# Values later in each pass, and the last row blocks' chains earlier, in a two-layer attention and MLP kernel bound by ScalarE's exponentials

## The chip, the cores and the metric

One core of one Trainium2 chip. The metric is the time of one execution on the device in microseconds (us). Every execution also comes with the span of the core (from its first to its last instruction, about 1.8 us less) and its mean granted TensorE clock. All executions here are in the fast state; they still differ by some us, and much of this document is about why.

## The reference

Two layers of the same weights, each an attention and an MLP with residuals, over x of 2048 x 448 in bf16, 16 heads of 28:

```python
x = x + A(layernorm(x), wqkv, wo)     # softmax(q k^T / sqrt(28)) v, 16 heads, then @ wo
x = x + B(layernorm(x), w1, b1, w2, b2)   # relu(x @ w1 + b1)^2 @ w2 + b2, 448 -> 1792 -> 448
x = x + A(layernorm(x), wqkv, wo)
x = x + B(layernorm(x), w1, b1, w2, b2)
```

## The kernel before

The kernel is written as several streams of operations with a rank each. A planner in the program itself (it runs when the program is built) merges them into one fixed order per engine: of the operations that can start, the earliest, and at a tie the lower rank. So a constant moves thousands of instructions.

A *unit* is the scores of one head for 512 (key, query) columns in a PSUM bank. Three units fill a score tile (sc), and ScalarE takes their exponential in one instruction into a pt tile. VectorE takes a single unit now and then, by a polynomial of seven instructions (vi, vm, vh, pd). A *pass* is one group of four heads and one row block of 256 rows (128 in the last four blocks of the second layer). Its values are summed into one bank (oT), which VectorE then copies out to oT_sb (the *eviction*). When all four groups of a row block are done, its *chain* runs: projection, add to x, norm, MLP, add to x, store.

PSUM: two score tiles of three banks and two single banks. The single banks serve oT, the chain's matmuls (mt, tp), VectorE's units and *filler* (useless matmuls that keep TensorE busy).

```python
HEAT = 0.74        # filler matmuls when TensorE was busy for less than this
LASTP = 3.9        # rank of the last row block's chain
HOLD = 3           # values of a pass start at this many eighths of it
NPT = 11           # pt tiles
...
blocks = [[(0, 2), ..., (14, 2)], [(0, 2), ..., (10, 2), (12, 1), (13, 1), (14, 1), (15, 1)]]
...
def apart(i, now):                 # may VectorE take unit i?
    ...
    near = p_next[0] is not None and e_now[0] >= p_next[0] - NEAR_U
    want[0] = sum(r.when() is not None and r.when() <= now for r in R_m) < 1 + near
    return not want[0]             # not if too few single banks are free
...
def p_stream():                    # values, rank 2
    for pi, (l, qb, g, kbs, first, last) in enumerate(passes):
        ...
        hold = todo[0 if end else min(HOLD * len(todo) // 8, len(todo) - 1)]
        ...                        # wait until the scores of step `hold` have their exponentials
...
    if len(norm_done[l, qb]) == G:                       # V_PRIO, VectorE's exponentials: 3.8
        pl.spawn(LASTP if (l, qb) == (1, len(blocks[1]) - 1) else 4 + 0.1 * qb, chain(l, qb))
```

The softmax here doesn't subtract the row's maximum and nothing guards it: scores larger than these inputs give would overflow.

## Time and profile before

| | before |
|---|---|
| time, median of the first 3 runs | 939.75 us (939.41 to 942.1) |
| time, mean of 74 later runs | 939.95 us |
| span of the profiled run | 935.4 us, clock 0.993 |
| exponentials on ScalarE / units on VectorE | 663 / 59 |
| after ScalarE's last exponential | 22.6 us |

The lines that the prediction shows are not repeated. One more view is needed for later: ScalarE's timeline after its last exponential (start, duration, instruction, idle time before and what ended it).

```profile
912.91 0.60 ACT L897 ACTIVATE r<-sc 128x512 bf16<-128x512 f32 x1
...
914.63 0.59 ACT L421 COPY xnT<-sc 128x512 bf16<-128x512 bf16 x1
920.63 0.60 ACT L897 ACTIVATE r<-sc 128x512 bf16<-128x512 f32 x1 [5.41 <-PE sc L471]
921.69 0.59 ACT L421 COPY xnT<-tp 128x512 bf16<-128x512 bf16 x1 [0.46 <-PE tp L412]
```

Each xnT is the normed input of one row block's MLP. Two are made after the last exponential, and the first instruction belongs to a third block's MLP: three chains are still open when the exponentials end. In the trace, 136 first-layer and 42 second-layer matmuls start after that point.

### The profile page before, as it was taken

The numbers are of one execution on the slowest core, as the hardware profiler recorded it, in microseconds if no ns is written. First come the engines' busy times: TensorE is split into PE (matmuls) and PEld (weight loads), VectorE is DVE, ScalarE is ACT, GpSimd is POOL, SyncE is SP. The second block draws the span as 40 slices with busy tenths as digits, with TensorE's granted clock in tenths as the row PEclk, the third lists the DMA queues.
The fourth block names the chain that finished last, engine by engine and source line by source line (L and its number), as shares of the span: only waits on it lengthen the run. The fifth ranks groups of instructions, "written<-read, shape, count | busy, mean of one in ns | idle before, by whom it ended". The sixth has DMA issues, their size and how long they took to land.

```text
span 935.4 us, 28412 instructions
## 1 busy us (share of the span) xinstructions
PE 831.2 (89%) x12637; PEld 440.7 (47%) x12637; DVE 615.7 (66%) x1291; ACT 905.0 (97%) x683; POOL 41.3 (4%) x84
## 2 busy tenths in 40 slices
PE   8999878899888898888989999789888999888888
PEld 4555434344444444444445444444344444545556
DVE  6755676666677776766678564667677476666565
ACT  5999999999999999999999999999999999999992
POOL 4100000100000000000000000000000000000000
PEclk9999999999999999999999999999999999999999
DMA  9000010000000000000000000011000000000100
GB/s 277 10 2 1 3 43 13 13 9 13 14 10 12 13 14 8 13 14 1 1 2 2 1 2 2 14 38 30 18 14 18 18 18 18 17 22 12 25 11 16
DMA packets 34471, 18.39 MB, mean 20 GB/s; under 512 B 18474, under 2 KB 33899, under 8 KB 34348
## 3 DMA queue, kind: packets, MB, share of 16 engines
q1 hardware_dynamic: 34348, 16.58, 6.4%
q8 instruction: 98, 1.61, 0.7%
q14 instruction: 25, 0.20, 0.1%
HBM read 14.26 MB, written 2.07 MB: 17 GB/s over the span
## 4 chain that ended last, share of the span: by engine, by line
ACT 72%; issue 14%; PE 13%; DVE 1%; POOL 0%; ACTq 0%; DVEq 0%
ACT pt L663 72%; PE mt L471 4%; PE sc L645 3%; PE oT L766 2%; PE sc L471 2%; PE mt L281 1%; PE mt L946 1%; PE tp L412 0%; DVE x_sb L861 0%; DVE vh L698 0%; ACT Q_sb L486 0%; POOL rstd L393 0%; DVE xn L438 0%; DVE vi L676 0%; DVE xnT L423 0%
## 5 line engine op out<-in xcount | busy, mean ns | idle before, releaser
L663 ACT ACTIVATE pt<-sc 128x1536 bf16<-128x1536 f32 x663 | 892.0, 1777 | 3.6 <-PE sc L645 3.1
L645 PE MATMUL sc<-Q_sb,K_sb 32*128 32x256 bf16 (+1 forms) x5082 | 285.2, 261 | 84.1 <-ACT pt L663 77.6
L645 PEld LDWEIGHTS <-K_sb 32*128 32x128 bf16 x5256 | 130.4, 92 | 261.6 <-issue 251.4
L766 PE MATMUL oT<-pt,V_sb 128*32 128x256 bf16 (+1 forms) x4476 | 159.0, 265 | 0.0
L471 PE MATMUL mt<-xnT,w 128*128 128x256 bf16 (+1 forms) x904 | 119.0, 268 | 5.0 <-DVE vi L676 3.0
L766 PEld LDWEIGHTS <-V_sb 128*32 128x32 bf16 x4608 | 91.5, 96 | 50.3 <-issue 45.6
L899 DVE TENSOR_SCALAR r<-mt 128x512 bf16<-128x512 f32 (+1 forms) x105 | 71.4, 680 | 48.1 <-PE mt L471 46.9
L471 PEld LDWEIGHTS <-w 128*128 128x128 bf16 x1008 | 79.5, 98 | 40.6 <-issue 31.8
L698 DVE SCALAR_TENSOR_TENSOR vh<-vh,vm 128x512 f32<-128x512 f32 x118 | 80.7, 684 | 1.4
L676 DVE TENSOR_SCALAR vi<-mt 128x512 int32<-128x512 f32 x59 | 40.8, 691 | 54.0 <-PE mt L645 53.9
L946 PE MATMUL mt<-xn,ident 128*128 128x448 bf16 x211 | 70.8, 359 | 3.6 <-DVE xn L438 1.4
L861 DVE TENSOR_TENSOR x_sb<-x_sb,mt 128x448 bf16<-128x448 bf16 x62 | 38.3, 618 | 48.5 <-PE mt L471 47.9
L471 PE MATMUL mt<-w,h 128*128 128x448 bf16 x224 | 53.7, 355 | 0.0
L392 POOL TENSOR_TENSOR ve<-mv,eps_t 128x2 f32<-128x2 f32 (+1 forms) x34 | 9.0, 264 | 873.1 <-DVE mv L374 801.2
L471 PE MATMUL mt<-w,V_sb 128*128 128x448 bf16 x196 | 46.5, 355 | 0.0
L789 DVE COPY oT_sb<-oT 128x256 f32<-128x256 f32 (+1 forms) x52 | 19.7, 379 | 37.1 <-PE oT L766 36.8
L703 DVE SCALAR_TENSOR_TENSOR pd<-vh,vi 128x512 bf16<-128x512 f32 x59 | 40.4, 685 | 0.7
L373 DVE BATCH_NORM_STATS2 st<-x_sb 128x6 f32<-128x448 bf16 x64 | 39.6, 619 | 1.3 <-DMA x_sb<-in_A_x_dram 0.6
L698 DVE SCALAR_TENSOR_TENSOR vh<-vm 128x512 f32<-128x512 f32 x59 | 40.2, 681 | 0.0
L492 DVE CAST K_sb<-mt 128x512 bf16<-128x512 f32 x30 | 20.7, 691 | 22.3 <-PE mt L471 22.1
L471 PE MATMUL mt<-xnT,wk 128*128 128x256 bf16 x240 | 34.1, 274 | 0.8 <-DVE vi L676 0.8
L471 PE MATMUL mt<-wo,oTn 128*128 128x448 bf16 x128 | 33.6, 368 | 0.4
(83 smaller groups left out, 643.4 us busy)
## 6 DMA issues: line engine op xcount, KB each, us to landing
rec<-scr SPq DMA_DIRECT2D x52, 128.0 KB
x_sb<-in_A_x_dram SPq DMA_DIRECT2D x8, 224.0 KB
out_dram<-x_sb SPq DMA_DIRECT2D x16, 112.0 KB
w<-in_B_w_dram SPq DMA_DIRECT2D x1, 1568.0 KB
w<-in_B_w_dram SPq DMA_DIRECT2D x1, 1344.0 KB
dn<-oT_sb SPq DMA_DIRECT2D x52, 4.0 KB
scr<-dn SPq DMA_DIRECT2D x52, 4.0 KB
rec<-scr SPq DMA_DIRECT2D x12, 64.0 KB
```

The costliest lines, as they stand in the source:

```text
L373: nc.vector.bn_stats(out=st[:, :], in_=x_sb[:, t0 + j, :])
L471: nc.tensor.matmul(box["t"][:, c0:c0 + n], lhsT=lhsT() if callable(lhsT) else lhsT, rhs=rhs, start=a, stop=b)
L492: nc.vector.tensor_copy(out=dst, in_=src)
L645: nc.tensor.matmul(dst[k][:, i * nt * P:(i + 1) * nt * P], lhsT=K_sb[l][rows, g, (kb + i) * P:(kb + i + 1) * P], rhs=Q_sb[rows, g, t0 * P: ...
L663: nc.scalar.activation(out=pt[:, 0:n], in_=gbuf[gi]["sc"][:, 0:n], func=AF.Exp, scale=float(np.log(2.0)) * 2.0 ** -23)
L676: nc.vector.tensor_scalar(out=box["i"][:, :], in0=src, scalar1=EXP_BIAS, scalar2=0.0, op0=ALU.add, op1=ALU.max)
L698: nc.vector.scalar_tensor_tensor(out=h[:, :], in0=src, scalar=b, in1=m, op0=ALU.add, op1=ALU.mult)
L703: nc.vector.scalar_tensor_tensor(out=pd[:, :], in0=h[:, :], scalar=b0, in1=i.bitcast(DT.float32), op0=ALU.add, op1=ALU.mult)
L766: nc.tensor.matmul(box["t"][DHP * hh:DHP * hh + DHP, 0:n], lhsT=V_sb[l][:, kb + i, 4 * g + hh, :], rhs=p[:, c0:c0 + n], start=begin and kb ...
L861: nc.vector.tensor_tensor(out=x_sb[:, tb, :], in0=x_sb[:, tb, :], in1=t[:, 0:D], op=ALU.add)
L899: nc.vector.tensor_scalar(out=r[:, 0:w], in0=t[:, 0:w], scalar1=0.0, scalar2=None, op0=ALU.max)
L946: nc.tensor.matmul(t[:, 0:D], lhsT=ident[:, :], rhs=xns[0][:, 0:D], start=True, stop=True)
```

## The change

The intent: hold the oT bank for a shorter time, so that chains and VectorE's exponentials find a free bank; and let the chains of the last row blocks go ahead of VectorE's exponentials, so that less of them is left at the end. By the edit this holds for three of the last four: they get ranks 3.4 to 3.6, below the 3.8 of VectorE's exponentials, while the last block's chain keeps 3.9, and so falls behind the other three, which it led before. Lines of the changed kernel stand five lower than those of the kernel before (L663 is L668).

```diff
-HOLD = 3
+HOLD = 5
+HOLD1 = 7
+NL = 4
+NLP = 3.8
+STOP = 0
+HSTOP = 0
...
-            hold = todo[0 if end else min(HOLD * len(todo) // 8, len(todo) - 1)]
+            hold = todo[0 if end else min((HOLD if nt == 2 else HOLD1) * len(todo) // 8, len(todo) - 1)]
...
-            pl.spawn(LASTP if (l, qb) == (1, len(blocks[1]) - 1) else 4 + 0.1 * qb, chain(l, qb))
+            pl.spawn(LASTP if (l, qb) == (1, len(blocks[1]) - 1) else NLP + 0.1 * (qb - len(blocks[1])) if l == 1 and qb >= len(blocks[1]) - NL else 4 + 0.1 * qb, chain(l, qb))
```

(Left out: STOP and HSTOP enter two conditions; at 0 they do nothing.)

More of the change, by code (lines that the diff above doesn't have):

```diff
@@ L588, in apart @@
         want[0] = False
-        if not LEAD <= len(gbuf) <= LAST or i + LAG > ends_at[units[i][0]]:
+        if len(units) - i < STOP or not LEAD <= len(gbuf) <= LAST or i + LAG > ends_at[units[i][0]]:
             return False
@@ L938, in heat @@
             short = HEAT - pl.load(WINDOW)
-            if short <= 0 or not s_left:
+            if short <= 0 or not s_left or len(units) - at[0] < HSTOP:
                 continue
```

## The prediction

> **What bounds the kernel now.** I read the page first (busy shares, then the groups), then the windows, then the timelines of ScalarE and VectorE at the end of the run.
>
> ```profile
> PE 831.2 (89%) x12637; PEld 440.7 (47%) x12637; DVE 615.7 (66%) x1291; ACT 905.0 (97%) x683; POOL 41.3 (4%) x84
> ...
> L663 ACT ACTIVATE pt<-sc 128x1536 bf16<-128x1536 f32 x663 | 892.0, 1777 | 3.6 <-PE sc L645 3.1
> ```
>
> ScalarE is busy 97% of a span of 935.4 us, and 892.0 us of its 905.0 are one group: 663 exponentials of 128x1536. A further 59 units of 128x512 get their exponential on VectorE (the group that writes pd, x59): 3 x 663 + 59 = 2048 units, all there are. TensorE's 89% is not a bound of the same kind: it is partly filler (211 matmuls of the identity, L946, and repeated score matmuls) and it waits 77.6 us for ScalarE by the list of waits.
>
> From the trace's records of the exponentials: the first ends at 17.2 us, the last at 912.8 us, and 650 of the 662 distances between successive ends average 1.343 us. So the span is 17.2 (start) + 662 x 1.343 = 889.3 + 6.3 lost + 22.6 (tail) = 935.4 us. Of the 6.3 us, 2.4 are in the start, at 25 to 28 us. The other 3.9 lie in four places, and the windows show what they have in common:
>
> ```profile
> 184.00:188.00 4.00, 3.83 (x47) 1.57 (x47) 0.69 (x4) 3.21 (x3) 0.00 (x0) 0.59 0.02 4
> 662.00:666.00 4.00, 4.00 (x31) 1.29 (x23) 3.03 (x7) 3.58 (x3) 0.00 (x0) 0.57 0.07 23
> 785.00:789.00 4.00, 4.00 (x50) 1.46 (x49) 1.25 (x3) 3.55 (x4) 0.00 (x0) 0.57 0.00 0
> 850.00:854.00 4.00, 3.73 (x65) 2.44 (x65) 2.56 (x6) 3.75 (x4) 0.00 (x0) 0.57 0.06 18
> ```
>
> The columns are busy time of PE, PEld, DVE, ACT, POOL, then the granted clock. In each the clock falls to 0.50 for 3.41 us, the scores come late, and ScalarE idles; from the exponentials' ends they cost 1.0, 1.3, 0.9 and 0.6 us. Each follows a quiet stretch of TensorE (busy 0.93 of 2.00 us at 180 to 182).
>
> The tail, from VectorE's timeline (start, duration, instruction):
>
> ```profile
> 915.21 0.29 DVE L789 COPY oT_sb<-oT 128x128 f32<-128x128 f32 x1
> ...
> 917.14 0.29 DVE L850 TENSOR_TENSOR oTn<-oT_sb,rec 128x128 bf16<-128x128 f32 x1
> 918.37 0.62 DVE L861 TENSOR_TENSOR x_sb<-x_sb,mt 128x448 bf16<-128x448 bf16 x1 [0.94 <-PE mt L471]
> 919.03 0.63 DVE L373 BATCH_NORM_STATS2 st<-x_sb 128x6 f32<-128x448 bf16 x1
> ...
> 929.22 0.62 DVE L861 TENSOR_TENSOR x_sb<-x_sb,sc 128x448 bf16<-128x448 bf16 x1 [1.40 <-PE sc L471]
> 932.06 0.62 DVE L861 TENSOR_TENSOR x_sb<-x_sb,sc 128x448 bf16<-128x448 bf16 x1 [2.22 <-PE sc L471]
> ```
>
> After the last exponential (912.8) it is one dependent chain: the last values, eviction at 915.21, reciprocal, output projection added at 918.37, norm, first MLP layer, second layer added at 932.06, store. The two adds at 929.22 and 932.06 are those of the last two row blocks: the chain of the last but one was still to do, and took TensorE from the last one.
>
> **What the Trainium skill says.** "ScalarE: Activation LUTs", section What ACT_TABLE_LOAD costs: an activation with immediate scale and bias takes 186 ns + 0.833 ns per element, and neighbours overlap by about 93 ns. For 1536 that is 1373 ns; the trace has 1343, which agrees, and 0.833 x 512 = 0.43 us is my estimate of what an exponential of 1024 saves. "TensorE: Matmul & The Clock Gate", section Part 1: The HAM clock gate: a free-running window of 3413 ns, and half clock after an idle one; the trace has four stretches of 3.41 us at 0.50, after windows busy only about half, so not fully idle ones. "PSUM — Partial Sum Buffer", section Specifications (TRN2): eight banks of 2 KiB. Here two score tiles take three each, so two single banks (mt, oT) serve values, chains, filler and VectorE's exponentials alike; no trace shows the size of PSUM, but the tiles' names show the sharing.
>
> **The change, part by part.** STOP and HSTOP are 0 and do nothing. The order of instructions of the two built programs gives the counts.
>
> *Values later.* A pass of 256 rows has 32 units, 10.7 exponentials, 14.3 us. Its oT bank was taken after 3/8 of them and held till eviction: between 100 and 500 us the median from the first value matmul to the eviction's end is 7.6 us. Starting at 5/8 removes 2/8 x 14.3 = 3.6 us of that, to about 4. A pass of 128 rows has 5.3 exponentials, 7.2 us; from its second of four steps to its last is half, another 3.6 us off a median of 4.4. The number of value matmuls stays at 4608. What the freed bank buys is that VectorE takes 63 units, not 59. ScalarE then has 661 exponentials of 1536 and one of 1024: 1 x 1.343 + 0.43 = **1.8 us less** on the bound. The four more on VectorE cost it some 4 x 4.0 us (0.69 + 0.42 + 0.42 + 4 x 0.68 = 4.25, pipelined a little), beside the bound: DVE is at 66%.
>
> *Filler.* 24 identity matmuls fewer (24 x 0.19 = 4.5 us), 105 repeated score matmuls more (at about 0.07 us, 7 us). TensorE's total grows by under 3 us, off the path.
>
> *Chains of the last four row blocks ahead of VectorE's exponentials.* Before, ScalarE had nine instructions of chains left after its last exponential, with two transposed inputs (xnT); after, five, with one. In TensorE's order only 15 second-layer matmuls of the last but one block are left behind the last value matmul; before, its whole first layer, too. I lay out the new tail with the old durations, E being the end of the last exponential. The last values need no wait for 56 first-layer matmuls any more (before: they ran at 914.53, 1.7 us after E); eviction at E + 0.8 (before E + 2.4). Then, however, the order puts the other block's 15 second-layer matmuls between the sum of denominators and the output projection. From eviction O: denominators until O + 0.9, 15 matmuls 2.85 us (926.18 to 929.02 in the old trace), projection 0.8, drain 0.2: the add starts at O + 4.75, where before it was O + 3.16. So 1.6 us are given back. Then add to xnT 3.9 us as before (918.37 to 922.28); 56 first-layer matmuls alone on TensorE at 0.056 us each, 3.2; last relu and square 1.4; second layer 3.05; add, store and its landing 3.3 (932.06 to 935.4). Sum: 0.8 + 4.75 + 3.9 + 0.1 + 3.2 + 1.4 + 3.05 + 3.3 = 20.5 us against 22.6: **2.1 us less**. One check: the last VectorE exponential. From its vi to its pd VectorE has 14 instructions of 8.0 us, and ScalarE from the same point 6 x 1.343 + 0.9 = 9.0 us less some 0.8 until vi starts, 8.2 us, so it ends just in time.
>
> *Lateness.* Bunching the values at the end of a pass loads TensorE unevenly. Charging each score, value and chain matmul with its old pace, 57 of the stretches from one score tile to the next hold over 1.6 us of TensorE work (before 38), and the greatest backlog, as an estimate from those paces, is 0.9 us (before 0.6) where a score may be about 0.9 late (1.343 less 0.4 for itself). I charge **0.5 us**.
>
> Sum: -1.8 - 2.1 + 0.5 = -3.4 us. 939.75 - 3.4 = 936.3, say **936.2 us**.
>
> **Rivals.** (1) *Clock dips decide.* They are worth 0.6 to 1.3 us each and depend on the phase of a free window, so four may be one or eight. For: the runs of before spread over 2.7 us, as much as the gain. With one dip the time would be 933, with eight, 940. By my sums, stretches of three score tiles with under 2.4 us of work go from six to eight, so slightly against us. (2) *Scores late behind the bunched values.* For: backlog 0.9 is the whole slack, and a half-clock stretch falling into such a bunch costs double. Against: ScalarE waits just 3.6 us for scores now. It would make 938 to 943. (3) *ScalarE waits for a buffer.* There are 11 pt tiles, and a pass now holds 8 before its first value matmul. For: three tiles are 4 us of slack, and a value step may wait for VectorE's share, 4 us and more. Against: no wait of ScalarE for oT exists now. If each of the 36 full passes of 256 rows lost 0.4 us, that is 14 us and the time 950. (4) *The tail gives nothing*, if the 15 matmuls and the last pd come later than I lay out: 938.
>
> **Range and chances.** The certain part is 1.8 us (counts). The tail is good for 0 to 4, dips for +-3, lateness for 0 to 4. In 8 of 10 cases I expect 931.8 to 940.8. Two per cent are 19 us: no term here comes near it, as the start, 660 exponentials at a fixed pace and a dependent tail remain. Faster by over 2%: 0.01; within: 0.98; slower: 0.01, for rival 3.
>
> **What would show it.** Right: 662 exponentials, pace 1.343; pd x63; hold of oT about 4 us; tail 20 to 21 us with the projection's add waiting for second-layer matmuls; no ACT wait for oT. Wrong: gaps between exponentials outside the half-clock stretches (rival 2), ACT waiting for PE's values (3), a tail of 22 us or more (4), or a number of half-clock stretches far from four (1). The prediction fails if the losses in mid-run come to under 1 or over 8 us.

## The result, and the profile after

| | before | after |
|---|---|---|
| time, median | 940.91 us (4 runs) | 935.56 us (4 runs, 934.47 to 936.68) |
| ratio | | 0.9944, 95% interval 0.9921 to 0.9967 |
| ratio when repeated (11 runs) | | 0.9954, 0.9937 to 0.9970 |
| span of the profiled run | 935.4 us, clock 0.993 | 934.9 us, clock 0.982 |

Ratios are the mean time of one kernel's fast runs over that of the other's of the same rounds, so not quite the ratio of the medians quoted. The change is 0.5% faster: inside the 2% band, inside the range, close to the predicted 936.2.

Yet the two profiles differ by only 0.5 us. Both numbers are right, and the clock tells why. The profiled run of before was one of its best (spans of its 74 later runs: 934.5 to 941.4, mean 938.0). From the page of the changed kernel:

```profile
PE 825.9 (88%) x12718; PEld 447.8 (48%) x12718; DVE 633.1 (68%) x1323; ACT 900.8 (96%) x678; POOL 41.5 (4%) x84
...
L668 ACT ACTIVATE pt<-sc 128x1536 bf16<-128x1536 f32 x662 | 890.3, 1739 | 6.3 <-PE sc L650 4.9
...
L708 DVE SCALAR_TENSOR_TENSOR pd<-vh,vi 128x512 bf16<-128x512 f32 x63 | 43.1, 685 | 1.7 <-PE oT L771 0.9
```

662 exponentials and 63 units on VectorE, as the order said. ScalarE's idle time ahead of exponentials rose from 3.6 to 6.3 us. The windows of the changed kernel (busy time of PE, PEld, DVE, ACT, POOL, then the granted clock) show where:

```profile
101.00:105.00 4.00, 3.62 (x52) 1.43 (x51) 2.82 (x6) 4.00 (x4) 0.00 (x0) 0.64 0.00 0
105.00:109.00 4.00, 4.00 (x45) 1.40 (x40) 2.06 (x4) 3.09 (x3) 0.00 (x0) 0.51 0.01 4
...
600.00:604.00 4.00, 3.73 (x45) 1.54 (x47) 3.00 (x6) 3.39 (x4) 0.00 (x0) 0.57 0.03 2
```

Before had four half-clock stretches of 3.41 us. This run has eight before the last exponential, three pairs (the first from 102.1 to 108.9 us) and two single ones. From the ends of the exponentials, the eight cost 5.9 us (before: four, 3.8 us), and all other gaps after the start 0.9 us.

The tail is the second surprise. VectorE's timeline, to be held against that of before in the prediction:

```profile
914.34 0.29 DVE L794 COPY oT_sb<-oT 128x128 f32<-128x128 f32 x1 [0.94 <-PE oT L771]
...
916.21 0.29 DVE L855 TENSOR_TENSOR oTn<-oT_sb,rec 128x128 bf16<-128x128 f32 x1
918.05 1.38 DVE L866 TENSOR_TENSOR x_sb<-x_sb,sc 128x448 bf16<-128x448 bf16 x2 [1.55 <-PE sc L476]
919.46 0.63 DVE L378 BATCH_NORM_STATS2 st<-x_sb 128x6 f32<-128x448 bf16 x1
...
931.57 0.62 DVE L866 TENSOR_TENSOR x_sb<-x_sb,mt 128x448 bf16<-128x448 bf16 x1 [1.88 <-PE mt L476]
```

The last exponential ends at 913.63. The eviction follows after 0.71 us (before 2.39). Then the two adds stand together: the other block's second layer and the last block's projection, the latter starts at 918.81, 4.47 us after the eviction (before 3.16), about as laid out. But from the input of the last MLP to its end TensorE is slow. Its timeline:

```profile
917.85 0.92 PE L476 MATMUL sc<-wo,oTn 128*128 128x448 bf16 x4
921.69 0.61 PE L417 MATMUL tp<-ident,xn 128*128 128x128 bf16 x4 [2.92 <-DVE xn L443]
922.97 1.87 PE L476 MATMUL mt<-xnT,w 128*128 128x128 bf16 x16 [0.67 <-ACT xnT L426]
924.63 3.62 PE L476 MATMUL sc<-xnT,w 128*128 128x128 bf16 x32
928.05 0.65 PE L476 MATMUL mt<-xnT,w 128*128 128x128 bf16 x8
928.53 0.35 PE L476 MATMUL mt<-b2w,one 128*128 128x448 bf16 x1
```

The 56 first-layer matmuls take 5.7 us from 922.97, not 3.2, after 2.92 us in which TensorE waited for the norm. The windows give the clock:

```profile
918.00:921.00 3.00, 0.77 (x5) 0.20 (x2) 2.05 (x4) 0.00 (x0) 0.54 (x2) 1.00 0.11 38
921.00:925.00 4.00, 2.63 (x24) 2.48 (x25) 0.40 (x1) 0.71 (x2) 0.20 (x1) 0.54 0.00 0
925.00:928.00 3.00, 3.00 (x31) 3.00 (x29) 0.85 (x2) 1.07 (x2) 0.00 (x0) 0.50 0.00 0
```

TensorE was busy for 0.77 of 3 us, and then it ran at half clock from 921.3 to 928.1 us: two stretches right in the last dependent chain. ScalarE's timeline shows that only one MLP input is made after the last exponential, where there were two:

```profile
913.74 0.38 ACT L902 ACTIVATE r<-sc 128x256 bf16<-128x256 f32 x1
922.34 0.59 ACT L426 COPY xnT<-tp 128x512 bf16<-128x512 bf16 x1 [8.22 <-PE tp L417]
924.88 0.60 ACT L902 ACTIVATE r<-mt 128x512 bf16<-128x512 f32 x1 [1.95 <-PE mt L476]
```

56 first-layer and 28 second-layer matmuls are left for after that point, against 136 and 42.

So the profiled pair balances to: start -0.3, exponentials -1.8, gaps between exponentials +2.9, tail -1.3, sum -0.5 us. The mean of many runs says -4.2 us of span (933.8 for 15 runs, 938.0 for 74). To compare kernels, the chance in the clock has to be taken out.

**Counting half-clock stretches in every run.** Each run's mean clock is on record, so (1 - clock) x span x 2 / 3.413 is its number of half-clock stretches. An estimate, by least squares over the 185 runs of all kernels here but hold7_lastp (one free constant for each kernel, one common slope): a stretch costs 0.79 us, standard error 0.04. The constant, the span with no stretch at all, is an extrapolation and called *fixed span* below: before 932.0, after 926.2 us, errors of 0.3 to 0.5. The change takes 5.9 us off the fixed span and adds 2.1 stretches (7.6 to 9.7 a run), 1.6 us; the sum is the measured -4.2. The common slope is a simplification: fitted one by one, the kernels' slopes run from 0.24 (cap59) to 1.24 (heat85), further apart than their errors (0.06 to 0.32) allow, and the own fits of before and after give 930.8 and 925.9 us, 4.9 apart with an error of 1.5. So fixed spans are good to about 1 us, not to 0.3.

### The profile page after: what moved, and what is told of

Same layout as the page of the kernel before. It is cut to its first block, busy times and chain, and to the rows that moved or that the text cites. A ratio compares the mean times of both kernels' runs of the same rounds, so it can differ in the third digit from the quotient of the medians.

```text
span 934.9 us, 28645 instructions
## 1 busy us (share of the span) xinstructions
PE 825.9 (88%) x12718; PEld 447.8 (48%) x12718; DVE 633.1 (68%) x1323; ACT 900.8 (96%) x678; POOL 41.5 (4%) x84
## 4 chain that ended last, share of the span: by engine, by line
ACT 69%; issue 17%; PE 10%; DMA 2%; DVE 1%; SPq 0%; POOLq 0%; POOL 0%; ACTq 0%
ACT pt L668 69%; PE sc L650 3%; PE mt L476 3%; DMA dn<-oT_sb 2%; PE oT L771 1%; PE sc L476 1%; PE mt L286 1%; PE mt L951 1%; PE tp L417 0%; DVE vh L703 0%; DVE st L378 0%; DVE x_sb L866 0%; DVE oT_sb L796 0%; DVE vi L681 0%; DVE dn L838 0%
## 5 line engine op out<-in xcount | busy, mean ns | idle before, releaser
L668 ACT ACTIVATE pt<-sc 128x1536 bf16<-128x1536 f32 x662 | 890.3, 1739 | 6.3 <-PE sc L650 4.9
L650 PE MATMUL sc<-Q_sb,K_sb 32*128 32x256 bf16 (+1 forms) x5194 | 292.3, 264 | 88.7 <-ACT pt L668 84.1
L771 PE MATMUL oT<-pt,V_sb 128*32 128x256 bf16 (+1 forms) x4468 | 153.6, 266 | 0.6 <-ACT pt L668 0.6
L476 PE MATMUL mt<-xnT,w 128*128 128x256 bf16 (+1 forms) x968 | 122.8, 265 | 5.2 <-DVE vi L681 1.6
L771 PEld LDWEIGHTS <-V_sb 128*32 128x32 bf16 x4608 | 94.6, 97 | 45.4 <-issue 40.8
L904 DVE TENSOR_SCALAR r<-mt 128x512 bf16<-128x512 f32 x110 | 74.6, 678 | 47.1 <-PE mt L476 46.3
L476 PEld LDWEIGHTS <-w 128*128 128x128 bf16 x1008 | 82.3, 100 | 40.4 <-issue 31.4
L703 DVE SCALAR_TENSOR_TENSOR vh<-vh,vm 128x512 f32<-128x512 f32 x126 | 86.2, 684 | 1.7
L951 PE MATMUL mt<-xn,ident 128*128 128x448 bf16 x187 | 63.1, 369 | 1.6 <-DVE xn L443 0.9
L443 DVE TENSOR_SCALAR xn<-x_sb,mv,rstd 128x448 bf16<-128x448 bf16 x64 | 23.5, 391 | 14.5 <-POOL rstd L398 14.1
L476 PE MATMUL mt<-xnT,wq 128*128 128x256 bf16 x240 | 33.1, 274 | 0.1
```

Source lines behind the costliest of these rows:

```text
L443: nc.vector.tensor_scalar(out=xn[:, 0:D], in0=x_sb[:, t0 + j, :], scalar1=mv[0][:, j, 0:1], scalar2=ln["r"][:, j:j + 1], op0=ALU.subtract, ...
L476: nc.tensor.matmul(box["t"][:, c0:c0 + n], lhsT=lhsT() if callable(lhsT) else lhsT, rhs=rhs, start=a, stop=b)
L650: nc.tensor.matmul(dst[k][:, i * nt * P:(i + 1) * nt * P], lhsT=K_sb[l][rows, g, (kb + i) * P:(kb + i + 1) * P], rhs=Q_sb[rows, g, t0 * P: ...
L668: nc.scalar.activation(out=pt[:, 0:n], in_=gbuf[gi]["sc"][:, 0:n], func=AF.Exp, scale=float(np.log(2.0)) * 2.0 ** -23)
L703: nc.vector.scalar_tensor_tensor(out=h[:, :], in0=src, scalar=b, in1=m, op0=ALU.add, op1=ALU.mult)
L771: nc.tensor.matmul(box["t"][DHP * hh:DHP * hh + DHP, 0:n], lhsT=V_sb[l][:, kb + i, 4 * g + hh, :], rhs=p[:, c0:c0 + n], start=begin and kb ...
```

## The experiments

Each is the changed kernel with the edit shown. Twelve runs were made beside the kernel before, in three calls on one chip each; each call has its own runs of the kernel before (24, 15 and 35). All results were correct.

| kernel | runs | median us | ratio to before (95%) | exponentials | stretches a run | fixed span | tail in its profile |
|---|---|---|---|---|---|---|---|
| before | 74 | 939.2, 940.9, 940.1 | 1 | 663 | 7.6 | 932.0 | 22.58 |
| after_again | 11 | 935.53 | 0.9954 (0.9937 to 0.9970) | 661 + 2/3 | 9.7 | 926.2 | 21.19 |
| chains_only | 14 | 939.58 | 0.9998 (0.9984 to 1.0012) | 663 | 7.0 | 931.7 | 22.60 |
| hold_only | 6 | 933.10 | 0.9929 (0.9903 to 0.9956) | 661 + 2/3 | 7.2 | 926.0 | 21.03 |
| hold128_only | 10 | 935.69 | 0.9951 (0.9930 to 0.9972) | 663 | 7.3 | 928.1 | 19.00 |
| hold256_only | 6 | 932.70 | 0.9932 (0.9907 to 0.9956) | 662 + 1/3 | 7.4 | 926.2 | 18.39 |
| cap59 | 11 | 936.46 | 0.9953 (0.9937 to 0.9970) | 663 | 8.7 | 927.4 | 19.49 |
| tail_warm | 6 | 932.24 | 0.9924 (0.9901 to 0.9946) | 661 + 2/3 | 7.7 | 924.8 | 18.63 |
| lastp | 6 | 933.14 | 0.9920 (0.9897 to 0.9944) | 661 + 2/3 | 9.5 | 924.0 | 18.90 |
| lastp_warm | 6 | 931.68 | 0.9916 (0.9888 to 0.9945) | 661 + 2/3 | 7.5 | 924.3 | 17.30 |
| heat85 | 9 | 936.03 | 0.9955 (0.9938 to 0.9972) | 665 | 1.6 | 932.5 | 19.41 |
| hold6_both | 22 | 937.40 | 0.9976 (0.9964 to 0.9989) | 660 + 2/3 | 11.0 | 927.2 | 19.64 |
| hold7_lastp | 5 | 978.59 | 1.0411 (1.0385 to 1.0437) | 659 + 2/3 | 18.9 | not fitted | 22.37 |

(The row after_again has the 11 runs of that call; its stretches and fixed span are those of all 15 runs of the changed kernel.)

The tails, cut at their dependent steps, in us; the half clock column is what overlaps the tail in that profile:

| | last exponential to eviction | to projection's add | to MLP input | to last square | to last add | to end | half clock |
|---|---|---|---|---|---|---|---|
| predicted | 0.8 | 4.75 | 3.9 | 4.7 | 3.05 | 3.3 | none |
| before | 2.39 | 3.16 | 3.91 | 5.54 | 4.24 | 3.34 | none |
| after | 0.71 | 4.47 | 4.12 | 6.77 | 1.88 | 3.34 | 6.8 us |
| chains_only | 1.39 | 7.77 | 3.89 | 4.33 | 1.88 | 3.33 | none |
| hold_only | 3.12 | 2.83 | 3.90 | 5.96 | 1.88 | 3.33 | 3.4 us |
| hold128_only | 2.73 | 2.83 | 3.90 | 4.33 | 1.88 | 3.33 | none |
| hold256_only | 0.47 | 2.86 | 4.26 | 4.64 | 2.82 | 3.34 | none |
| tail_warm | 0.71 | 4.47 | 3.90 | 4.33 | 1.88 | 3.34 | none |
| lastp | 0.71 | 3.14 | 3.91 | 5.93 | 1.88 | 3.34 | 3.4 us |
| lastp_warm | 0.71 | 3.14 | 3.90 | 4.33 | 1.88 | 3.34 | none |

### The changed kernel again

No edit.

> The changed kernel once more, beside the kernel before on one chip. Sum of the prediction: 1.8 us from 1.33 exponentials fewer and 2.1 us from the tail, less half-clock stretches. Rival: the gain is mostly that the kernel before falls into more half-clock stretches in ordinary runs than in the one profiled. The first expects a ratio near 0.996 and mean granted clocks alike in both kernels; the rival a ratio of 0.994 and a clock of before under 0.98.

Measured: 0.9954, clock 0.982 on average over its 15 runs, 0.986 for before. Neither expectation fits as it was put. The kernel before does not lose more to half-clock stretches in ordinary runs than the changed one: it loses less. It only has more of them in ordinary runs than in the one that was profiled. The gain is therefore in the fixed part, and larger than it looks.

### One half of the change at a time

```diff
-NL = 4
+NL = 0        # hold_only: chains in their old rank
```

> Only the values later, chains of the last row blocks in their old rank. By its order it has 661 exponentials of 1536 and one of 1024, as the full change, but the first layer of the last but one row block still stands before the last values. The sum expects 1.8 us off and a tail of some 22.6 us, so a ratio of 0.998. If the later values are the whole gain: 0.994.

```diff
-HOLD = 5
-HOLD1 = 7
+HOLD = 3      # chains_only: values at three eighths in all passes
+HOLD1 = 3
```

> Only the last four row blocks' chains ahead of VectorE's exponentials, values at three eighths as before. By its order 663 exponentials and 59 on VectorE as before, and in the tail the last block's projection stands behind the other block's whole first layer, so the tail should be longer than 22.6 us, by 1 to 3 us: ratio 1.001 to 1.003. If the ranks alone shorten the tail by 2.1 us: 0.998.

Measured: 0.9929 and 0.9998. The later values alone are the whole gain; the ranks alone are worth nothing. chains_only's tail is 22.60 us, to 0.02 us that of before, by another road. VectorE's timeline of chains_only:

```profile
914.27 0.29 DVE L794 COPY oT_sb<-oT 128x128 f32<-128x128 f32 x1
...
922.05 0.61 DVE L866 TENSOR_TENSOR x_sb<-x_sb,sc 128x448 bf16<-128x448 bf16 x1
```

The projection of the last block, ready to run from about 916, is added at 922.05: its chain now comes last of the four (rank 3.9 against 3.4 to 3.6), and the other blocks' first layers go ahead of it. I had expected that (1 to 3 us longer); what I missed is that the rest of the tail then runs alone and wins back as much. Whether the ranks cost something within the full change is not settled: hold_only is ahead of after_again (933.1 and 935.5 us), but with overlapping intervals, equal fixed spans (926.0 and 926.2) and 2.5 stretches fewer. By the cut tails at full clock the ranks take another 0.8 us off the later values' tail: 19.40 us in hold_only (21.03 less 1.63 for its half clock) against 18.63 in tail_warm. That is one profile each.

### Which passes

```diff
-HOLD = 5
-NL = 4
+HOLD = 3      # hold128_only: later only in the last four row blocks' 16 passes
+NL = 0
```

> Only the passes of 128 rows (the last four row blocks) begin their values at the end; passes of 256 at three eighths and the ranks as before. 663 exponentials and 59 on VectorE as before. If the gain of the later values comes from the exponentials moved, nothing: ratio 1.000. If it comes also from the tail, where the last passes are of 128 rows: 1 to 1.5 us, ratio 0.9985, tail about 21 us.

```diff
-HOLD1 = 7
-NL = 4
+HOLD1 = 3     # hold256_only: later only in passes of 256 rows
+NL = 0
```

> Only the passes of 256 rows begin their values at five eighths; the last ones at three eighths and the ranks as before. By its order 662 exponentials of 1536 and one of 512, 61 on VectorE, so 0.67 of an exponential fewer: 0.9 us. In its tail two transposed inputs are left after the last exponential, as before: 22.6 us. Ratio 0.999. If later values as such take ScalarE's waits away, more: 0.996.

Measured: 0.9951 and 0.9932, where I expected at best 0.9985 and 0.996. hold128_only is the clearest of all: it has the same 663 exponentials, the same 59 units on VectorE and the same ranks as before, and is 0.5% faster. The end of VectorE's timeline of hold128_only:

```profile
918.21 0.62 DVE L866 TENSOR_TENSOR x_sb<-x_sb,mt 128x448 bf16<-128x448 bf16 x1 [0.61 <-PE mt L476]
...
928.32 0.62 DVE L866 TENSOR_TENSOR x_sb<-x_sb,sc 128x448 bf16<-128x448 bf16 x1 [1.88 <-PE sc L476]
```

From the projection's add to the last add it takes 10.1 us; before, 918.37 to 932.06, 13.7. The 3.6 us are the whole difference of the two tails, and of the fixed spans (3.9). In the last 16 passes the oT bank is held for a median of 1.4 us, not 4.4, and when the last exponential ends, 94 first-layer and 28 second-layer matmuls are left, not 136 and 42. So later values shorten the tail with no exponential moved. That the free bank is what lets the chains run earlier is how the program is built and fits these counts; no run here changed the number of banks, so this link is argued.

hold256_only moves 0.67 of an exponential (0.9 us) and has a tail 4.2 us shorter; the sum, 5.1, is near its fixed 5.9 us. Both parts of the later values shorten the same tail, so they do not add: together they have a fixed gain of 6.0.

### What the moved exponentials are worth

```diff
+CAP = 59
-        if len(units) - i < STOP or ...
+        if sum("x" in b for b in gbuf) >= CAP or len(units) - i < STOP or ...
```

> The changed kernel, but VectorE takes no unit after its 59th, as many as before: 663 exponentials on ScalarE. All else of the change stays until the last stretch, where the order also changes. If the moved exponentials are worth their count, 1.33 x 1.343 = 1.8 us lost against the changed kernel: ratio to before 0.997. If they are worth nothing since later values gain by the tail alone: 0.995.

Measured: 0.9953, like the changed kernel, so by time alone the moved exponentials look worthless. But its tail changed too. It is 19.49 us with one half-clock stretch (to the last square 5.96, not 4.33), so 17.9 at full clock, 0.8 less than tail_warm's. The fixed span is 1.2 us longer than the changed kernel's; with 0.8 gained in the tail that makes 2.0 for 1.33 exponentials, where the count says 1.8. But the 1.2 hangs on the common slope, and cap59's own is far from it (0.24). So what the moved exponentials are worth is not shown by a run; it is a count times a measured pace.

### The half clock in the tail

```diff
+        if (l, qb) == (1, len(blocks[1]) - 1):       # tail_warm: TAIL = 14
+            def filler(e):
+                t = bank(wm, "mt")
+                for _ in range(TAIL):
+                    nc.tensor.matmul(t[:, 0:D], lhsT=ident[:, :], rhs=b2w[:, :], start=True, stop=True)
+            wm = Op("PE", 0.19 * TAIL, filler, acq=pools_now())
+            yield wm
+            yield Op("PE", 0.0, None, deps=[wm], rel=wm)
         xnT, own_xt, ends = yield from layernorm(t0, nt, None, mv=mv)
```

> The changed kernel with 14 matmuls of zeros into a free bank between the last projection and the last transposes, where TensorE stood idle from 918.8 to 921.7 us. Nothing else of the order changes but bank names in the tail. If that idle stretch causes the half clock of the tail, the clock stays full there, the last first layer takes 3.2 us, not 5.5, and the kernel is 2.4 us faster than the changed one: ratio to before 0.993, tail 18.9 us. If the half clock has another cause: as the changed kernel, 0.995 to 0.996, tail 21.3 us.

(All but one row of the filler's operand b2w are zero, not all.) Measured: 0.9924. TensorE's timeline of tail_warm:

```profile
915.18 0.92 PE L477 MATMUL sc<-wo,oTn 128*128 128x448 bf16 x4
915.94 2.81 PE L888 MATMUL mt<-b2w,ident 128*128 128x448 bf16 x14
919.02 0.40 PE L418 MATMUL tp<-ident,xn 128*128 128x128 bf16 x4 [0.27 <-DVE xn L444]
920.09 1.95 PE L477 MATMUL sc<-xnT,w 128*128 128x128 bf16 x32 [0.67 <-ACT xnT L427]
921.87 1.50 PE L477 MATMUL mt<-xnT,w 128*128 128x128 bf16 x24
```

Useless work in the idle stretch, and the 56 first-layer matmuls take 3.3 us, not 5.7. The tail is 18.63 us against 21.28, the runs have 7.7 stretches on average against 9.7. Two stretches fewer, as the two at 921.3 say. The averages alone (errors 0.7 and 0.4) would be weak evidence. Of the other profiles, eight leave TensorE idle for 1.2 us or more just ahead of the last transposes: six of them have half clock behind it, hold128_only and heat85 have not. The two with filler there have none. So the idle wait was a cause of the half clock in the tail, shown; that it always brings half clock is not: heat85 has the same 2.92 us, split between two windows of 3.41 us that are 47 and 48% busy.

```diff
-LASTP = 3.9
+LASTP = 3.3   # lastp: the last row block's chain ahead of the other three
```

> The changed kernel with the last row block's chain ranked ahead of the others (3.3 for 3.9). Its order differs in the tail alone: the four projection matmuls stand after 7 of the other block's 14 second-layer matmuls, not after all, and the other 7 fill TensorE's idle stretch. If the half clock in the changed kernel's tail (921.3 to 928.1 us) comes from that idle stretch, both go: projection 1.4 us earlier and first layer 2.4 us shorter, 3.8 us off the changed kernel, tail 17.5 us. If the half clock stays: 1.4 us off.

The intent of the change was undone in one place: with ranks of 3.4 to 3.6 for the others and 3.9 for the last, the block that ends the program yields to the one before it. With 3.3 the order differs in the tail alone. Measured: 0.9920, by medians 2.4 us ahead of after_again. The projection's add came 3.14 us after the eviction, not 4.47, as expected; one of two half-clock stretches was left in its profile (923.3 to 926.7), so it lies between the two outcomes.

```diff
-LASTP = 3.9
+LASTP = 3.3   # lastp_warm: and the filler above, TAIL = 7
```

> Both mends of the tail together: the last row block's chain first, and seven filler matmuls in the gap that is left before the last transposes. If the half clock after an idle stretch and the late projection are separate costs (2.4 and 1.4 us), this is faster than either mend alone: tail 17.4 us, ratio to before 0.990. If the two mends remove the same cost: 0.992, as each alone.

Measured: tail 17.30 us, as expected, in the profile; 0.9916 in time. That is the fastest kernel here, 0.4% ahead of the changed one, but lastp and tail_warm are within its interval. That both mends add up is shown by the cut tails, not by the times.

### Filler against exponentials

```diff
-HEAT = 0.74
+HEAT = 0.85   # heat85
```

> The changed kernel with the filler's threshold at 0.85 for 0.74. By its order 665 exponentials and 53 on VectorE: 3.3 exponentials more than the changed kernel, 4.5 us. If half clock stretches come from quiet stretches of TensorE, their number falls from 9.7 a run to 5 or fewer, 4 us back at 0.86 us each: ratio 0.995, clock 0.99 or higher. If they do not depend on filler: ratio 1.000, clock 0.982.

Measured: 0.9955, as expected. The summary of the profiled run of heat85:

```profile
core 0: 931.6 us, clock 1.000
```

No half-clock stretch before its last instruction, 1.6 a run instead of 9.7. But filler takes the single banks too, so VectorE gets 53 units and not 63, ScalarE has 3.3 exponentials more, and the fixed span grows by 6.3 us (4.5 of it, by count, those exponentials); 8.0 stretches at 0.79 give 6.3 back. An even trade.

### Later still

```diff
-HOLD = 5
+HOLD = 7      # hold7_lastp; with LASTP = 3.3
```

> A version meant to beat both: values at seven eighths in all passes, ranks of the change with the last row block first (3.3). By its order 659 exponentials of 1536 and one of 1024, 69 on VectorE: 2 exponentials of 1536 fewer than the changed kernel with its last rank mended (2.7 us). If the moved exponentials count and bunched values cost nothing: ratio 0.989. If the bunching makes scores late or ScalarE waits for a pt buffer: 0.992 or worse, with waits of ScalarE outside half-clock stretches.

```diff
-HOLD = 5
+HOLD = 6      # hold6_both; with LASTP = 3.3 and the filler, TAIL = 7
```

> The same with the values of passes of 256 rows at six eighths. By its order 660 exponentials of 1536 and one of 1024, 66 on VectorE: one exponential fewer than the changed kernel, 1.3 us. In the kernel at seven eighths ScalarE waited 37.7 us for value matmuls, as a pass then holds 10.7 pt tiles of 11. At six eighths it holds 8 to 9.3: if that leaves enough slack, no such wait, ratio 0.989; if not, such waits in part of the 36 full passes, ratio 1.000 or more.

Measured: 1.0411 and 0.9976. The group of exponentials and the list of waits of hold7_lastp:

```profile
L668 ACT ACTIVATE pt<-sc 128x1536 bf16<-128x1536 f32 x660 | 891.1, 1608 | 44.9 <-PE oT L771 37.7 <-PE sc L650 7.2
```

```profile
ACT pt L668 <- PE oT L771: 37.7, 31, 3.0
```

A wait that did not exist before: 31 times ScalarE stood, 1.2 us on average, until value matmuls freed a pt tile. This is the prediction's third rival, at a later point than the change's. At six eighths the wait is nearly absent (2.0 us in two places), and one exponential more is saved, but the kernel is slower than lastp_warm: 11.0 stretches a run instead of 7.5, and a fixed span 2.8 us longer. In its profile the tail is 2.3 us longer, since the last but one block's first layer stands before the last values again, and 1.5 us of gaps lie outside half clock. Of the values tried, five eighths is the best.

## Why the prediction was right, and where it was not

- **The bound and the counts: right.** 662 exponentials at a pace of 1.343 us, 63 units on VectorE, 1.8 us off. The Trainium skill's "ScalarE: Activation LUTs" (section What ACT_TABLE_LOAD costs) gives an estimate of 0.43 us for the 512 elements saved in the last one; it ends 0.92 us after its predecessor, 0.42 under the pace. That the freed bank is what gave VectorE the four units is not separated: HOLD also moves `p_next`, and with it the point (`near`) from which VectorE needs two free banks. The hold itself fell less than laid out in passes of 256 rows, to a median of 5.0 us between 100 and 500 us (before 7.8 by the same count), not 4.
- **The tail: a term mis-sized, and its cause put in the wrong place.** I put -2.1 us on the part "Chains of the last four row blocks ahead of VectorE's exponentials". That step failed: chains_only has a tail of 22.60 us and no gain. (Nor do all four go ahead: the last keeps 3.9, behind 3.8.) The tail is shortened by the later values (hold128_only, 3.6 us), in which I saw only moved exponentials. In size, at full clock the gain is 4.0 us (22.58 to 18.63). Too long in my sum was the stretch from the MLP's input to the last add: 7.75 us laid out, 6.21 measured, since the last second layer does not wait for the last square. The term for the late projection (4.75, measured 4.47) held.
- **Half clock in the tail: not foreseen.** I laid out the idle stretch of TensorE and did not ask what follows it. It gives back 2.4 us (the last 56 first-layer matmuls took 5.7 us, not 3.3), and 0.2 more at the transposes, so that the tail gained 1.3 us in the profile.
- **Lateness, 0.5 us: about right.** Gaps outside half-clock stretches came to 0.9 and 0.1 us in two profiles of the changed kernel.
- **Net.** -1.8 - 4.0 = -5.8 against a fixed -5.9 (-4.9 by the two kernels' own fits, so that the close match may be luck); +1.6 for 2.1 more stretches; -4.2 in span. I had -3.4. By luck too the sum came out well: a tail gain put at half its size met a clock loss that was not in the sum.
- **Rivals.** (1) the half clock set the spread, as said, but I left its mean at four: in ordinary runs it is 7.6 before and 9.7 after, and the profiles have two of these in the tail. (2) did not show (the line above). (3) is real, at seven eighths, not at five. (4) is refuted.

## What to carry to other kernels

Before comparing two profiles, ask whether either is an ordinary run: here the list of spans and clocks of all runs settled in a minute what the two traces could not. When an engine is full, look at what is left after its last instruction: that dependent chain decided more than the instructions taken off the engine. In such a chain an idle TensorE is not free, because the wait can set the clock for the work that ends the program (2.4 us here); and ranks meant to bring work forward must put the piece that ends last first.

## What the Trainium skill lacked or had wrong

- "TensorE: Matmul & The Clock Gate", Part 1: The HAM clock gate: it tells of half clock after at least one idle window of about 3.4 us, and that gaps over 3.4 us are to be avoided; its section A second HAM failure mode adds that frequent micro-idles can do it, but gives no share of busy time. Here partly busy windows do it: the 3.41 us ahead of each of the four onsets in the profile of before hold matmul records for 47, 53, 54 and 56% of their time; of the six onsets in the profile after, five have 59 to 64% and the one in the tail 26%, with 2.92 us as the longest wait. Fully idle is not needed. All stretches of a run start whole multiples of 3.413 us apart, to 0.01 us; of the other windows on this grid at full clock, the quietest that were not followed by half clock hold 59 and 61% before, 61 and 62% after. So the border, by matmul records, is about 60% in these two profiles, and not sharp: in the tail of heat85 two windows of the grid with 47 and 48% were not followed by half clock, nor was one with 52% in hold128_only.
- The same page has one rule for the cost, throttled time x (1 - K/N) (section Terms), by which an estimate for 3.41 us at half clock is 1.7 us. It has no figure for a kernel that TensorE does not bound: here 0.79 us by the fit, and 2.4 us (of 3.4) for a pair that falls on a dependent chain.
- The same section's period of 3413 ns and the two clock states agree: every stretch in the profiles is 3.41 us or a multiple.
- "ScalarE: Activation LUTs", What ACT_TABLE_LOAD costs: an estimate of 1373 ns from its figures for successive exponentials of 1536, 1343 measured. The records' durations are of no use for this: by an estimate from the same figures one takes 1466 ns, and they run from 1444 to 1990, with a mean of 1777 ns at a pace of 1343.
